# All half units of float64 weights loaded as 128 rows, through more staging slots

## The chip, the cores and the metric

The kernel runs on one core of one Trainium2 chip. The core has TensorE (matmuls), VectorE, ScalarE and GpSimd (elementwise work), SyncE (SP here, which issues most transfers) and 16 DMA engines. In the profile they are called PE (with PEld for the weight loads of TensorE), DVE, ACT, POOL and SP. Instructions of one engine run in the order in which they stand on it. The metric is the device time of one launch in microseconds, the median of several runs; lower is better.

## What is computed

Three layers in a row, in float32, for 8 batches of 576 tokens with 8 heads of 64:

```python
a = softmax over the sequence of phi            # 32 memory slots per head
k_m, v_m = a^T @ k, a^T @ v
x = softmax(q @ k_m^T / 8) @ v_m                # attention on the slots
h = x @ moe_w_in                                # 4608 x 512 times 512 x 2048
x = (h * sigmoid(1.702 * h)) @ moe_w_out        # 2048 x 512
# then, by token, the expert e of 8 with the highest logit of x @ w_gate:
y = gate * sigmoid(x @ w_output_gate)[e] * (relu(x @ w1[e]) @ w2[e])
```

`moe_w_in` and `moe_w_out` come as float64, which the inputs' making leaves them in; the kernel reads their bytes and makes float32 of them itself. All other inputs are float32.

## The kernel before

Tokens lie in 16 halves of 288 columns, two for each batch, written (b, hf). The first feed-forward layer is cut into 16 **units** (`u` or `f`, 128 of the 2048 hidden columns each). One **step** is one unit for one half: six matmuls into `h` (`ffn_h`), a tanh gate on ScalarE and VectorE with a split of the result `g` into a rounded part and a rest (lines 367 to 370), and twelve matmuls into four accumulators `acc` (`ffn_out`); every product is made of three matmuls with such split operands. `emit_h` runs two steps ahead of `emit_out` (`LOOK`). The output projection of attention is folded into the weights of each batch (`project`, lines 341 to 346).

The list `steps` begins with four early segments, in which halves (0,0), (0,1), (1,0) and (1,1) go through units 0 to 5 (`CUT`); each ends with `evac` (lines 387 and 389) and a store of the partial sums, `partd`. Then each of the four halves goes through units 6 to 15, then come the other batches with all 16 units, then the expert layer, whose weights `w2` (float32) are loaded two ahead by `load2` and split by `split2`.

The float64 weights come in 32 **half units** of 128 x 2048 16-bit words, 512 KB each, numbered in the order in which they are loaded. `conv_load(n)` issues the load of half unit n on SP. `conv_slot(n)` converts n and n + 1: ScalarE takes the top words (line 195, one instruction for each of the two), VectorE builds the exponent and the mantissa and adds them (lines 196 to 212); for n % 4 of 2 or more, which holds `moe_w_out`, the raw tile itself takes the result, ScalarE rounds it (214) and GpSimd makes the rest (215). So raw tiles of n % 4 below 2 come free with line 211 on VectorE, the others with line 215 on GpSimd. Of the slots from 24 on, the temporaries are three tiles named `phi0`, `phi1` and `c0` in turn. Slot n must be done before the step of its units; `conv` paces the slots at 0.8 half units a step.

The raw words are read from a byte offset of one word, so that the last row of the last half unit would end one word behind the array; half unit 31 is therefore loaded as 127 rows (line 181) and one row of 2047 words (line 183).

Where raw tiles lie: half units 0 to 11 in four places of the buffers that later hold the units of group 2 (`stage(2, 2 + n % 4)`, called `wb_123` in the rows below), 12 to 31 in a ring of three tiles `stg`. The ring also takes the keys and values of the batches from 2 on, and later `w2`. The keys and values of batch 1 lie in group 3 (`stage(3, c)`, `wb_119`), which is taken by units 12 to 15 only later; group 3 also holds temporaries of the slots below 24. `conv_slot` ends with the loads ahead:

```python
        while loaded[0] < min(NV, n + (6 if n + 5 < NR else 5)):
```

The order on each engine is not the order of the code: a list scheduler of the program's framework moves instructions forward or back on their engine. It also adds the waits for data and for free buffers.

Of the kernel before, what the change touches and what calls it, by code (L numbers as in the profile page):

```python
# [37 lines left out]
OUT_SHAPE = (N, DM)  # L38
CH = [(0, 128), (128, 128), (256, 128), (384, 128), (512, 64)]
LOOK = 2  # L40
LEAD = 8
FE = 60
CV0 = (0, 4, 8)
NR, NT = 12, 24
O1, R1, OQ, RQ, OR, RR = 0, 0.5, 6, 0.4, 9, 0.6
S1 = 32
ORDER = 'p k0 k1 c0 k2 k3 c1 k4 q0 c2 w q1'
# [5 lines left out]
def tile_kernel(ctx: ExitStack, tc: tile.TileContext, phiT, kv, qT, w1, w2, wg, out):  # L53
    nc = tc.nc
    PS = bass.MemoryType.PSUM
    w1 = w1.bitcast(U16).rearrange("u a p n -> (u a p n)")

    const = ctx.enter_context(tc.tile_pool(name="const", bufs=1))
    sb = ctx.enter_context(tc.tile_pool(name="sb", bufs=2))
# [88 lines left out]
    def load_kv(b, c):  # L148
        s0, n = CH[c]
        if b < 2:  # L150
            t = stage(2, 6) if (b, c) == (0, 4) else stage(3, c)
        else:
            t = sb.tile([128, 1024], F32, name="stg", bufs=3)
        nc.sync.dma_start(out=t[:n], in_=kv[b, s0:s0 + n])
        kv_t[b, c] = t

# [15 lines left out]
    def conv_load(n):  # L172


        if n < NR:
            raw_t[n] = stage(2, 2 + n % 4).bitcast(U16)
        else:
            raw_t[n] = sb.tile([128, 2048], U16, name="stg", bufs=3)
        o = (2 * (2 * (n // 4) + n % 2) + n % 4 // 2) * 128 * 2048 + 1
        rows = 128 if n < NV - 1 else 127  # L180
        nc.sync.dma_start(out=raw_t[n][:rows], in_=w1[o:o + rows * 2048].rearrange("(p n) -> p n", p=rows))
        if rows < 128:
            nc.sync.dma_start(out=raw_t[n][rows:, :2047], in_=w1[o + rows * 2048:o + 128 * 2048 - 1].rearrange("(p n) -> p n", p=1))

    def conv_slot(n):


        if n < NT:
            top, t = (stage(3, 5 + (n + i) % 6 / 2, 512).bitcast(U16) for i in range(2))
        else:  # L190
            top, t = (sb.tile([128, 1024], U16, name=("phi0", "phi1", "c0")[(n + i) % 3], bufs=1) for i in range(2))
        raw = [raw_t.pop(n + i) for i in range(2)]
        tops = [x.rearrange("p (n b) -> p n b", b=4)[:, :, 2] for x in raw]
        for i in range(2):
            nc.scalar.activation(out=t.bitcast(BF16)[:, 512 * i:512 * i + 512], in_=tops[i].bitcast(BF16), func=AF.Abs)
        nc.vector.tensor_scalar(out=t.bitcast(BF16), in0=t.bitcast(BF16), scalar1=WLO, scalar2=WHI,
                                op0=ALU.max, op1=ALU.min)
        nc.vector.tensor_scalar(out=t, in0=t, scalar1=3, scalar2=0x3FFF,
                                op0=ALU.logical_shift_left, op1=ALU.bitwise_and)
        for i in range(2):  # L200
            h = slice(512 * i, 512 * i + 512)
            nc.vector.scalar_tensor_tensor(out=top[:, h], in0=tops[i], scalar=0xC000, in1=t[:, h],
                                           op0=ALU.bitwise_and, op1=ALU.bitwise_or)
        nc.vector.tensor_scalar(out=t, in0=top, scalar1=0xFF80, scalar2=None, op0=ALU.bitwise_and)
        for i in range(2):
            h = slice(512 * i, 512 * i + 512)
            u = 2 * (n // 4) + i
            wa, wb = (x[:, u % 4] for x in group(u // 4, "A"))
            m = raw[i].bitcast(U32).rearrange("p (n b) -> p n b", b=2)[:, :, 0]
            w = wa if n % 4 < 2 else m.bitcast(F32)  # L210
            nc.vector.scalar_tensor_tensor(out=w, in0=m, scalar=2.0 ** -36, in1=t.bitcast(BF16)[:, h], op0=ALU.mult, op1=ALU.mult)
            nc.vector.tensor_add(out=w, in0=w, in1=top.bitcast(BF16)[:, h])  # L212
            if n % 4 >= 2:
                nc.scalar.copy(out=wb[:, 512:1024], in_=w)  # L214
                nc.gpsimd.tensor_sub(out=wb[:, 1024:1536], in0=w, in1=wb[:, 512:1024].bitcast(F32))
                u_t[u] = (wb[:, 0:256], wb[:, 256:512]), (wb[:, 512:1024], wb[:, 1024:1536])
        while loaded[0] < min(NV, n + (6 if n + 5 < NR else 5)):
            conv_load(loaded[0])
            loaded[0] += 1

# [1 line left out]
    stg_t = {}  # L222

    def load2(key, src):
        stg_t[key] = sb.tile([128, 1024], F32, name="stg", bufs=3)
        nc.sync.dma_start(out=stg_t[key], in_=src)

    def split2(key, slot):
# [354 lines left out]
    def slot_tasks():  # L583
# [39 lines left out]
        def g(i):  # L623
            p = misc([128, 4, SLOT], 1 - i)
            for j in range(4):
                nc.tensor.transpose(p[:, j], st["h"][:, i, j], ident)
            t = sb.tile([128, 2, 4, SLOT], F32R, name="stg", bufs=3)
            nc.scalar.copy(out=t[:, 0], in_=p)
            nc.vector.tensor_sub(out=t[:, 1], in0=p, in1=t[:, 0].bitcast(F32))
            st["g", i] = t  # L630
# [50 lines left out]
    def spread(step, thunks, every=1):  # L681
        for i, t in enumerate(thunks):
            put(int(step + i * every), t)
# [50 lines left out]
    def attn_tasks():  # L734
        for b in range(B):
# [8 lines left out]
            if b + 1 < B:  # L744
# [13 lines left out]
                else:  # L758
                    put(O1, lambda n=n: load_phi(n), lambda n=n: load_q(n, 0))
                    for c in range(5):  # L760
                        put(O1, lambda n=n, c=c: load_kv(n, c))
                    spread(O1, cm, R1)
                    spread(O1 + OQ, q0, RQ)

    def project_tasks():
# [111 lines left out]
def host(q, k, v, phi, moe_w_in, moe_w_out, moe2_w_gate, moe2_w_output_gate, moe2_w1, moe2_w2):  # L877
# [14 lines left out]
        a = wi.reshape(KD, 128, f, 128).transpose(2, 1, 0, 3).reshape(f, 128, 512)  # L892
        return np.concatenate([a, wo.reshape(f, 128, 512)], axis=2)

    w1 = c(units(moe_w_in, moe_w_out).reshape(NF1, 128, 2, 512).transpose(0, 2, 1, 3)).view(np.int64)
    w2 = c(np.stack([units(moe2_w1[e], moe2_w2[e]) for e in range(E)]))
    wg = c(np.concatenate([moe2_w_gate, moe2_w_output_gate], axis=1).reshape(KD, 128, 16).transpose(1, 0, 2))
    return dict(phiT=phiT, kv=kvp.reshape(B, S, H * 2 * D), qT=qTp, w1=w1, w2=w2, wg=wg)
# [21 lines left out]
```

## Time and profile before

| | |
|---|---|
| median of three runs | 1280.32 us (1278.87 to 1280.46) |
| profiled execution, its own time | 1287.78 us |
| its span, first to last instruction | 1286.1 us |
| mean granted clock of TensorE | 0.963 of full |

The rows that follow further below come from the profiled execution. A row of the timeline has start and duration in us, engine, line, operation, output <- input, and in brackets how long the engine sat idle before it and what ended that. "x12" means so many instructions in one merged row. L12 is line 12 of the kernel before; of the changed kernel, lines from 176 on are one to nine further down.

### The profile page before, as it was taken

What the parts mean: (1) busy time and instruction counts of PE and PEld (TensorE: products, weight loads), DVE (VectorE), ACT (ScalarE), POOL (GpSimd) and SP (SyncE); (2) the same over time, 40 slices, a digit from 0 to 9 for tenths busy, and PEclk for the clock granted to TensorE, in tenths of its full rate; (3) what the DMA queues carried; (4) which work ended last, traced back from release to release, by engine and by line L of the source; (5) the groups of instructions that cost most, each with busy time, mean ns of one, the idle gap of its engine ahead of it and who ended that gap; (6) DMA issues with size and microseconds to landing.
All of it is one profiled execution on the core that took longest, in us unless ns stands there. A gap on an engine that the chain in (4) does not pass through costs nothing. (4 is left out here: it accounts for less than half of the span.)

```text
span 1286.1 us, 24689 instructions
## 1 busy us (share of the span) xinstructions
PE 1196.4 (93%) x9628; PEld 1107.5 (86%) x9628; DVE 742.4 (58%) x2011; ACT 497.7 (39%) x1144; POOL 133.9 (10%) x137
## 2 busy tenths in 40 slices
PE   4689737999999999999999999999999999999996
PEld 2478626888988988999889889989999999999995
DVE  5898726576466467466556546676463553544521
ACT  3445414344444444443443444553242332332410
POOL 1221000020100100101101102001110001001100
PEclk8689967999999999999999999999999999999998
DMA  8534313433311311401311310475453443534300
GB/s 297 193 107 122 131 63 95 126 80 88 108 42 56 112 39 56 130 20 56 130 38 38 119 31 20 107 230 150 130 162 95 136 156 85 171 103 123 116 23 22
DMA packets 77017, 132.00 MB, mean 103 GB/s; under 512 B 12738, under 2 KB 49730, under 8 KB 76898
## 3 DMA queue, kind: packets, MB, share of 16 engines
q1 hardware_dynamic: 75170, 130.25, 33.2%
q8 instruction: 76, 1.25, 0.4%
q14 instruction: 43, 0.35, 0.1%
q0 software_dynamic: 1728, 0.15, 0.1%
HBM read 99.65 MB, written 31.12 MB: 102 GB/s over the span
## 5 line engine op out<-in xcount | busy, mean ns | idle before, releaser
L352 PE MATMUL acc<-g,wb 128*128 128x288 f32 x4608 | 690.1, 298 | 13.5 <-ACT wb L214 6.2
L352 PEld LDWEIGHTS acc<-g,wb 128*128 128x128 f32 x4608 | 642.6, 191 | 22.1 <-ACT g L369 6.8
L352 PE MATMUL h<-x,wb 128*128 128x288 f32 x2560 | 478.0, 305 | 36.6 <-DVE g L370 24.2
L352 PEld LDWEIGHTS h<-x,wb 128*128 128x128 f32 x2560 | 386.4, 191 | 86.1 <-issue 30.7
L367 ACT ACTIVATE th<-h 128x288 f32<-128x288 f32 x256 | 105.0, 411 | 122.0 <-PE h L352 121.4
L352 PE MATMUL h<-x,wa 128*128 128x288 f32 x512 | 151.5, 296 | 0.0
L369 ACT CAST g<-th 128x288 fp32r<-128x288 f32 x196 | 84.9, 433 | 171.2 <-PE acc L352 149.0
L370 DVE TENSOR_TENSOR g<-th,g 128x288 fp32r<-128x288 f32 x196 | 88.8, 453 | 100.2 <-ACT g L369 99.9
L368 DVE SCALAR_TENSOR_TENSOR th<-th,h 128x288 f32<-128x288 f32 x196 | 87.8, 448 | 75.5 <-ACT th L367 74.6
L373 DVE SCALAR_TENSOR_TENSOR g<-h,g 128x288 fp32r<-128x288 f32 x128 | 58.0, 453 | 117.3 <-ACT g L372 116.9
L231 ACT CAST wb<-stg 128x1024 fp32r<-128x1024 f32 x72 | 75.6, 1050 | 105.5 <-PE acc L352 90.4
L372 ACT ACTIVATE g<-h 128x288 fp32r<-128x288 f32 x128 | 52.2, 408 | 162.9 <-PE acc L352 162.0
L352 PEld LDWEIGHTS h<-x,wa 128*128 128x128 f32 x512 | 96.8, 189 | 0.0
L232 DVE TENSOR_TENSOR wa<-stg,wb 128x512 fp32r<-128x512 f32 x72 | 51.5, 715 | 77.4 <-ACT wb L231 76.9
L578 POOL TENSOR_TENSOR rt<-rt,scl 128x1152 f32<-128x1152 f32 x15 | 33.6, 2241 | 352.5 <-DVE rt L404 252.4
L330 POOL TENSOR_TENSOR x<-sf,x 128x288 fp32r<-128x288 f32 x32 | 25.9, 808 | 420.7 <-ACT x L329 394.4
L514 POOL DMA_INDIRECT listd<-ids,pos x48 | 45.5, 948 | 188.8 <-DVE ssm L321 67.4
L233 DVE TENSOR_TENSOR wb<-stg,wb 128x512 fp32r<-128x512 f32 x72 | 57.0, 792 | 0.0
L341 PE MATMUL m<-wa,kvc 64*32 64x512 f32 (+1 forms) x592 | 42.2, 576 | 10.7 <-DVE wa L212 9.3
L346 DVE TENSOR_TENSOR wb<-m,wb 128x512 fp32r<-128x512 f32 (+1 forms) x74 | 42.3, 608 | 15.7 <-ACT wb L345 15.7
L345 ACT CAST wb<-m 128x512 fp32r<-128x512 f32 (+1 forms) x74 | 35.6, 529 | 17.9 <-PE m L341 17.7
L369 ACT CAST g<-h 128x288 fp32r<-128x288 f32 x60 | 23.9, 398 | 46.6 <-PE acc L352 30.0
(200 smaller groups left out, 811.1 us busy)
## 6 DMA issues: line engine op xcount, KB each, us to landing
stg<-in_w_dram SPq DMA_DIRECT2D x91, 512.0 KB, 4.0
stg<-in_kv_dram SPq DMA_DIRECT2D x24, 512.0 KB, 4.0
x2d<-x SPq DMA_DIRECT2D x16, 576.0 KB, 5.9
x2tok<-rt SPq DMA_DIRECT2D x64, 144.0 KB, 2.9
x<-x2d SPq DMA_DIRECT2D x16, 576.0 KB, 4.0
out_dram<-rt SPq DMA_DIRECT2D x64, 144.0 KB, 2.8
q<-in_qT_dram SPq DMA_DIRECT2D x15, 576.0 KB, 3.9
wb<-in_w_dram SPq DMA_DIRECT2D x12, 512.0 KB, 4.8
```

What stands on the lines that cost most here:

```text
L231: nc.scalar.copy(out=wb[:, 0:1024], in_=stg)
L232: nc.vector.tensor_sub(out=wa, in0=stg[:, 0:512], in1=wb[:, 0:512].bitcast(F32))
L233: nc.vector.tensor_sub(out=wb[:, 1024:1536], in0=stg[:, 512:1024], in1=wb[:, 512:1024].bitcast(F32))
L346: nc.vector.tensor_sub(out=lo, in0=p[e], in1=hi.bitcast(F32))
L352: nc.tensor.matmul(p, lhsT=w[a][:, c0:c0 + 128], rhs=x[c], start=(first and i == 0), stop=(last and i == 2))
L367: nc.scalar.activation(out=t, in_=p, func=AF.Tanh, scale=0.851)
L368: nc.vector.scalar_tensor_tensor(out=o, in0=t, scalar=1.0, in1=p, op0=ALU.add, op1=ALU.mult)
L369: nc.scalar.copy(out=g[:, 0], in_=o)
L370: nc.vector.tensor_sub(out=g[:, 1], in0=o, in1=g[:, 0].bitcast(F32))
L372: nc.scalar.activation(out=g[:, 0], in_=p, func=AF.Relu)
L373: nc.vector.scalar_tensor_tensor(out=g[:, 1], in0=p, scalar=0.0, in1=g[:, 0].bitcast(F32), op0=ALU.max, op1=ALU.subtract)
L514: nc.gpsimd.indirect_dma_start(out=listd, out_offset=bass.IndirectOffsetOnAxis(ap=st["pos"][:, c:c + 1], axis=0), in_=ids[:, 2 * b * NJ + ...
```

## The change

All half units are loaded with 128 rows by one transfer. For that the host appends one word of float64 (a copy of the first) to the weights, so the last row can be read to its end; line 183 goes. The ring `stg` has four tiles instead of three (`NS`). Half units 0 to 15 now go through the places of group 2 (`NR` 16 instead of 12), 16 to 19 through the places of group 3 that held the keys and values of batch 1, and 20 to 31 through the ring. Loads from 16 on may be written out from step 5 on, when that batch's keys and values have been used (`free`); at that point all up to 23 are issued at once.

```diff
+NS = 4
-NR, NT = 12, 24
+NR, NT = 16, 24
...
-    w1 = w1.bitcast(U16).rearrange("u a p n -> (u a p n)")
+    w1 = w1.bitcast(U16)
...
         if n < NR:
             raw_t[n] = stage(2, 2 + n % 4).bitcast(U16)
+        elif n < NR + 4:
+            raw_t[n] = stage(3, n % 4).bitcast(U16)
         else:
-            raw_t[n] = sb.tile([128, 2048], U16, name="stg", bufs=3)
+            raw_t[n] = sb.tile([128, 2048], U16, name="stg", bufs=NS)
         o = (2 * (2 * (n // 4) + n % 2) + n % 4 // 2) * 128 * 2048 + 1
-        rows = 128 if n < NV - 1 else 127
-        nc.sync.dma_start(out=raw_t[n][:rows], in_=w1[o:o + rows * 2048].rearrange("(p n) -> p n", p=rows))
-        if rows < 128:
-            nc.sync.dma_start(out=raw_t[n][rows:, :2047], in_=w1[o + rows * 2048:o + 128 * 2048 - 1].rearrange("(p n) -> p n", p=1))
+        nc.sync.dma_start(out=raw_t[n], in_=w1[o:o + 128 * 2048].rearrange("(p n) -> p n", p=128))
...
-        while loaded[0] < min(NV, n + (6 if n + 5 < NR else 5)):
+        conv_loads(n + 6)
+
+    def conv_loads(n):
+
+        while loaded[0] < (min(NV, max(n, NR + 4 + NS)) if "free" in raw_t else min(n, NR)):
             conv_load(loaded[0])
             loaded[0] += 1
...
                     spread(O1, cm, R1)
+                    put(O1 + 5, lambda: raw_t.update(free=True), lambda: conv_loads(done[0] + 4))
...
-    w1 = c(units(moe_w_in, moe_w_out).reshape(NF1, 128, 2, 512).transpose(0, 2, 1, 3)).view(np.int64)
+    w1 = units(moe_w_in, moe_w_out).reshape(NF1, 128, 2, 512).transpose(0, 2, 1, 3).reshape(-1)
+    w1 = np.concatenate([w1, w1[:1]]).view(np.int64)
```

In the other places where the ring is named, `bufs=3` becomes `bufs=NS`.

The scheduler then orders the engines otherwise in the part where weights are converted. On SP, from the loads after batch 1's keys and values on, there stood before (`wb_123` are places of group 2, `stg` is the ring):

```order
L120 DMA listd<-x_525 128x288
L181 DMA stg<-in_w_dram 128x2048 x2
L181 DMA wb_123<-in_w_dram 128x2048 x2
L181 DMA stg<-in_w_dram 128x2048 x3
L704 DMA partd_0_102<-ev 128x1152
L162 DMA q<-in_qT_dram 128x1152
```

and in the changed kernel, with `wb_119` for group 3:

```order
L121 DMA listd<-x_525 128x288
L183 DMA stg<-in_w_dram 128x2048 x2
L183 DMA wb_123<-in_w_dram 128x2048 x2
L183 DMA stg<-in_w_dram 128x2048 x2
L183 DMA wb_123<-in_w_dram 128x2048 x4
L183 DMA wb_119<-in_w_dram 128x2048 x4
L708 DMA partd_0_102<-ev 128x1152
L163 DMA q<-in_qT_dram 128x1152
```

Before, the seven loads are half units 12 and 13, 10 and 11, 14 to 16. Now there are fourteen ahead of the first store of partial sums: 20 and 21, 10 and 11, 22 and 23, then 12 to 15 and 16 to 19, each behind the release of its place.

On ScalarE, around the steps of units 4 and 5 of the first early segment, there stood before (L367 and L369, the tanh and the cast of `g`; L258, copies for batch 1's attention):

```order
L367 ACTIVATE th<-h 128x288
L258 COPY et<-m_601 128x256
L367 ACTIVATE th<-h 128x288
L258 COPY et<-m_617 128x256
L369 CAST g<-h 128x288
L258 COPY et<-m_655 128x256
L369 CAST g<-h 128x288
L258 COPY et<-m_668 64x256
L367 ACTIVATE th<-h 128x288
L369 CAST g<-h 128x288
```

and now:

```order
L373 CAST g<-h 128x288
L262 COPY et<-m_615 128x256
L371 ACTIVATE th<-h 128x288
L262 COPY et<-m_653 128x256
L195 ACTIVATE wa_118<-wb_123 128x512
L373 CAST g<-h 128x288
L262 COPY et<-m_666 64x256
L195 ACTIVATE wa_118<-wb_123 128x512
L371 ACTIVATE th<-h 128x288
L195 ACTIVATE wa_118<-wb_119 128x512
L373 CAST g<-h 128x288
```

Three first operations on half units (14, 15 and 16, at L195) have moved in among the casts and activations of these steps.

On ScalarE around the last evacuation of the early segments (L389 before) there stood before:

```order
L195 ACTIVATE phi_1436<-stg 128x512
L367 ACTIVATE th<-h 128x288
L389 ACTIVATE ev<-acc_1284 128x288
L389 ACTIVATE ev<-acc_1286 128x288
L369 CAST g<-h 128x288
L367 ACTIVATE th<-h 128x288
L214 CAST wb_1097<-stg 128x512
L345 CAST wb_1097<-m_1574 128x2x128
L214 CAST wb_1097<-stg 128x512
```

and now (L393 is that evacuation):

```order
L195 ACTIVATE phi_1430<-stg 128x512
L373 CAST g<-h 128x288
L195 ACTIVATE phi_1430<-stg 128x512
L371 ACTIVATE th<-h 128x288 x2
L393 ACTIVATE ev<-acc_1278 128x288
L393 ACTIVATE ev<-acc_1280 128x288
L214 CAST wb_1099<-stg 128x512 x2
L373 CAST g<-h 128x288
L349 CAST wb_1099<-m_1479 128x2x128
L349 CAST wb_1099<-m_1480 128x2x128
L373 CAST g<-h 128x288
L195 ACTIVATE phi_1548<-stg 128x512 x2
```

Both first operations of slot 24 (half units 24 and 25) now stand ahead of the evacuation, where before the one of 25 stood twelve instructions behind it; those of slot 26 follow after four casts and the two of slot 22 (L214).

## Rows read from the trace of the kernel before

**Rows 1.** The page: the span, and TensorE's busy time with the other engines'.
```profile
span 1286.1 us, 24689 instructions
PE 1196.4 (93%) x9628; PEld 1107.5 (86%) x9628; DVE 742.4 (58%) x2011; ACT 497.7 (39%) x1144; POOL 133.9 (10%) x137
```
**Rows 2.** Windows: length, busy us of PE, PEld, DVE, ACT, POOL; clock, DMA share, GB/s.
```profile
80.00:140.00 60.00, 54.44 (x439) 48.29 (x439) 53.19 (x125) 30.80 (x77) 8.84 (x8) 0.97 0.40 132
140.00:210.00 70.00, 36.35 (x242) 31.26 (x241) 35.14 (x75) 19.05 (x43) 7.70 (x6) 0.73 0.29 92
...
400.00:600.00 200.00, 199.44 (x1732) 181.31 (x1732) 124.14 (x406) 88.25 (x223) 19.17 (x22) 1.00 0.24 72
```
**Rows 3.** TensorE's waits, 20 to 215 us, then 80 to 138: total, times, longest.
```profile
PE h L352 <- DVE g L370: 24.2, 5, 18.9
...
PE h L352 <- DVE g L370: 4.4, 3, 2.1
```
**Rows 4.** Timeline of the tail: ScalarE, then VectorE and SP.
```profile
137.88 0.41 ACT L389 ACTIVATE ev<-acc 128x288 f32<-128x288 f32 x1
...
155.11 0.74 ACT L195 ACTIVATE phi<-stg 128x512 bf16<-128x512 bf16 x1 [1.95 <-DVE wa L212]
...
164.07 0.65 ACT L195 ACTIVATE c<-stg 128x512 bf16<-128x512 bf16 x1
168.48 0.67 ACT L195 ACTIVATE c<-stg 128x512 bf16<-128x512 bf16 x1 [3.75 <-DMA stg<-in_w_dram]
174.43 0.67 ACT L195 ACTIVATE phi<-stg 128x512 bf16<-128x512 bf16 x1 [5.28 <-DVE wa L212]
...
195.76 0.65 ACT L195 ACTIVATE phi<-stg 128x512 bf16<-128x512 bf16 x1 [19.39 <-DMA stg<-in_w_dram]
...
201.09 1.29 DVE L212 TENSOR_TENSOR stg<-stg,phi 128x512 f32<-128x512 f32 x2
...
173.01 8.59 SPq L183 DMA_DIRECT2D stg<-in_w_dram  x1
```
**Rows 5.** Windows: the same columns, while half unit 31 is on its way.
```profile
185.00:190.00 5.00, 0.00 (x0) 0.00 (x0) 0.00 (x0) 0.00 (x0) 0.00 (x0) 0.50 0.06 26
```
**Rows 6.** Line 181, issue to landing: all; issued 150 to 168; half units 12, 13.
```profile
DMA to landing us min/median/max: 3.5/4.8/11.5
...
DMA to landing us min/median/max: 3.5/3.8/4.2
...
DMA to landing us min/median/max: 7.5/7.8/8.2
```
**Rows 7.** Timeline: slot 26 on VectorE (first and last), its casts, GpSimd for slot 22.
```profile
157.54 0.43 DVE L196 TENSOR_SCALAR phi<-phi 128x1024 bf16<-128x1024 bf16 x1 [0.41 <-ACT phi L195]
...
162.18 1.29 DVE L212 TENSOR_TENSOR stg<-stg,c 128x512 f32<-128x512 f32 x2
...
162.90 1.26 ACT L214 CAST wb<-stg 128x512 fp32r<-128x512 f32 x2 [1.32 <-DVE stg L212]
...
142.77 2.58 POOL L215 TENSOR_TENSOR wb<-stg,wb 128x512 fp32r<-128x512 f32 x2 [19.08 <-ACT wb L214]
```
**Rows 8.** Timeline: output matmuls of TensorE at the lower and at the full clock.
```profile
164.99 5.40 PE L352 MATMUL acc<-g,wb 128*128 128x288 f32 x22 [0.53 <-POOL wb L215]
...
209.88 1.76 PE L352 MATMUL acc<-g,wb 128*128 128x288 f32 x12
```
**Rows 9.** Timeline of the first early segment: VectorE, GpSimd, then ScalarE.
```profile
62.96 1.29 DVE L211 SCALAR_TENSOR_TENSOR wa<-wb,wa 128x512 f32<-128x512 uint32 x2
...
70.32 4.05 POOL L215 TENSOR_TENSOR wb<-wb,wb 128x512 fp32r<-128x512 f32 x2 [10.32 <-ACT wb L214]
...
73.87 0.41 ACT L369 CAST g<-h 128x288 fp32r<-128x288 f32 x1
...
77.63 0.40 ACT L369 CAST g<-h 128x288 fp32r<-128x288 f32 x1 [1.19 <-PE acc L352]
...
80.24 0.85 ACT L389 ACTIVATE ev<-acc 128x288 f32<-128x288 f32 x2
```

More of the change, by code (lines that the diff above doesn't have):

```diff
@@ L152, in load_kv @@
         else:
-            t = sb.tile([128, 1024], F32, name="stg", bufs=3)
+            t = sb.tile([128, 1024], F32, name="stg", bufs=NS)
         nc.sync.dma_start(out=t[:n], in_=kv[b, s0:s0 + n])
@@ L224, in load2 @@
     def load2(key, src):
-        stg_t[key] = sb.tile([128, 1024], F32, name="stg", bufs=3)
+        stg_t[key] = sb.tile([128, 1024], F32, name="stg", bufs=NS)
         nc.sync.dma_start(out=stg_t[key], in_=src)
@@ L626, in g @@
                 nc.tensor.transpose(p[:, j], st["h"][:, i, j], ident)
-            t = sb.tile([128, 2, 4, SLOT], F32R, name="stg", bufs=3)
+            t = sb.tile([128, 2, 4, SLOT], F32R, name="stg", bufs=NS)
             nc.scalar.copy(out=t[:, 0], in_=p)
```

## The prediction

> **What bounds the kernel now.** I read the page first for the shares [rows 1]: TensorE is busy 93% of the span, so it is the bound on the whole; what can be won is where it stands still. The windows by stage say where that is [rows 2]: from 400 to 600 us it is busy 199.4 of 200 us at the full granted clock (the stages after it look alike), but only 54.4 of 60 us from 80 to 140 and 36.4 of 70 us from 140 to 210, there at a mean clock of 0.73. So the loss lies ahead of 210 us, while weights are still being converted, and what is taken out there reaches the end undiminished. Next the waits of that stretch [rows 3]: the longest of TensorE is 18.9 us for `g` from VectorE. The timeline shows what it stands behind [rows 4]: ScalarE's row at L195 for half unit 31 (the last) starts at 195.76 after 19.39 us of waiting for a load of weights, and ScalarE's work behind it, the activations of two steps, starts only then. While it waits, the DMA engines show a busy share of 0.06, one of sixteen, at 26 GB/s [rows 5]; the other loads of the same line land in 3.5 to 11.5 us with a median of 4.8 [rows 6]. The one thing that sets the late load apart is its 127 rows, with a remainder of one row, whose issue alone holds SP 8.6 us.
>
> I write "slot n" for the conversion of half units n and n+1, and T0 for the first evacuation (L389) of the fourth early segment, at 137.88 [rows 4]. From T0 on ten steps of half 0 of batch 0 follow, with units 6 to 15, and their end waits for slot 30.
>
> **The tail, from T0 to the end of slot 30.** In before slot 30's last VectorE operation ends at 201.09 + 1.29 = 202.38, which is T0 + 64.5. In the changed program I work it out anew.
>
> The load of 31 now has 128 rows like the others, so its 19.39 us go. That alone would not be all: in before slot 28 also waited 3.75 us for half unit 29, since with three slots it can be issued only when slot 26 has been read by GpSimd; and slot 24 came late, its second L195 after T0. In the order of after, both L195 of slot 24 stand ahead of T0 on ScalarE, and after T0 VectorE has left of it one TENSOR_SCALAR and the two pairs of L211 and L212: about 0.4 + 1.3 + 1.3, with two evacuations between, T0 + 4.
>
> What is late next is the load of 26 and 27. They take the ring's slots of 22 and 23, whose last reader is GpSimd at L215. By the order that work starts behind T0: two evacuations of 0.4 us on ScalarE, half of a 1.26 us pair of casts, then 2.58 us for two subtractions [rows 7], so 27 can be issued at T0 + 0.8 + 0.7 + 2.6 = T0 + 4.1; with 0.3 for the issue and 3.8 for landing (the median of the four loads between 150 and 168 us [rows 6]) and 0.7 for its L195, VectorE can start slot 26 at T0 + 9. So this load is a new wait of some 4 to 5 us on ScalarE, and `g` for the next step is queued behind it; I count it in full.
>
> A slot's chain on VectorE takes from 157.54 to 162.18 + 1.29, 5.9 us with the steps' operations between [rows 7]. Slot 26 then ends at T0 + 14.9. From there the slots are a serial chain, because three temporaries (`phi0`, `phi1`, `c0`) go round and each slot's second is the one before's result: the period is 6.0 + 0.7 = 6.7 us where the load was there (from 168.48 to 174.43 with the first L195) and 9.0 us where casts lay between (155.11 to 164.07) [rows 4, 7]. I take 7.7, about midway, as both kinds follow each other. Slot 28 ends at T0 + 22.6, slot 30 at T0 + 30.3. Loads 28 and 29 wait for slot 24 alone, 30 and 31 for GpSimd after slot 26, at about T0 + 19; landed by T0 + 23.4, they come just when ScalarE wants them. Against T0 + 64.5 the tail is **34.2 us shorter**; with the period at its ends (2.0 less or 2.6 more for two of them) and a landing of 3.5 to 4.8 us [rows 6], 30.6 to 36.5. TensorE itself permits it: twelve output matmuls take 1.76 us at full clock [rows 8], 0.147 each, so ten steps of 18 are 26 us, and some 30 with the projections that the order puts between them. The clock can add to the gain, up to 2 us, as the last two steps in before ran at half level.
>
> **The first stretch, up to T0.** Here the change costs. In before, half units 12 and 13 were fetched at 42.7 us into a free ring slot; now 12 to 15 go to group 2 again and wait for the slots of 8 to 11. Load 12 waits for slot 8's L211, at 62.96 + 0.7; it lands at about 68, and ScalarE stands at its L195. Loads 14 and 15 wait for GpSimd's pair from 70.32 to 74.37 [rows 9], a little later as 12 delays the pair (1 us): released at 73 and 75, landed at 77 and 79.5. By the order the L195 of 14 now stands ahead of a cast of `g` that in before ran at 73.87, that of 16 ahead of one that ran at 77.63. So the cast at 73.87 moves to about 78, and the one at 77.63 to 80.7 (16 landing soon behind 15) or to 84.5 (if four loads in a row take 7.5 to 8.2 us, as two loads behind others did [rows 6]). On SP, the transfers queued behind these waiting loads are 17 to 19, the `partd` store and the next `q`; none is wanted before the evacuation at 80.24. I take that evacuation 5 us later (4 to 7).
>
> From there to T0 nothing waits for a load: 16 to 23 are all in. In before TensorE lost 5.6 of 60 us between 80 and 140 [rows 2]. But VectorE is busy 53.2 of these 60, and by the order it has slot 24, 5.9 us, to do in part there besides. I give back 2 of the 5, so T0 is **3 us later** (from 2 earlier, 4 less all of the 5.6, to 9 later, 7 and a third of slot 24).
>
> By the Trainium skill it would be a little less: its page "DMA: Bandwidth & Descriptors", section "Anatomy of one DMA", puts a transfer at 2.0 us plus its bytes at 436 GB/s, an estimate of 3.2 us for 512 KB, though for transfers issued from GpSimd. The row of this case has 3.8 for the tail and the sum goes by that; by the page the wait for 27 and that for 15 would be 0.6 us shorter each.
>
> **The rest.** Two w2 loads ahead stay two loads ahead, so the fourth ring slot is worth nothing in the expert half by the order of issue; TensorE is full there [rows 2]. The appended word costs no instruction. Loads are as many as before, less the one-row remainder.
>
> **Sum.** -34.2 + 3 = -31 us. The profiled execution took 1287.78 us around a span of 1286.1; it would take 1256.6. The median of the three runs, 1280.32, is 7.5 us below that execution; shifted alike, 1249.
>
> **Rivals.**
> - *Only the 128 rows pay.* Load 31, issued just ahead of the row at 173.01 [rows 4], would land 3.8 us later instead of 23: -19. The ring's share of 15 is eaten if the period is 9.0, load 27 takes 7.8 us to land as 12 and 13 did [rows 6] and T0 comes 9 us late: -34.2 + 2.6 + 4 + 9 = -19, so 1261, from 1258 to 1264. For it speaks that VectorE has little room from 80 to 140; against it that the load waits of that stretch do go.
> - *The clock falls in the tail.* From 80 to 140 us the granted clock was 0.97 on the mean [rows 2] with no wait of TensorE above 2.1 us [rows 3]; in the tail with its long waits it was 0.73, and there, at the lower level of 1.2 GHz, 22 output matmuls took 5.40 us, 0.245 each, against 0.147 [rows 8]. Were all ten steps at the lower level, their 30 us would be about 50 and bind, where the forecast ends them some 5 us behind slot 30, at T0 + 35: 15 us of the gain go, 1264; with half of them at it, 40 us, 1254. The page "TensorE: Matmul & The Clock Gate" of the Trainium skill, section "Part 1: The HAM clock gate", says the slow level is the default and only activity lifts it; by that rule bursts parted by load waits stay slow. Against it: the one wait that I find is of 4 to 5 us, and TensorE is two steps behind ScalarE there.
> - *Slower: each load of the first stretch is waited for alone.* Loads 12 to 19 are eight; if ScalarE stood before each for a whole landing, 8 x 4.8 = 38 us [rows 6], it would give back more than 34.2 and end at about 1284. It decides from 4.3 us a load on. Against it: 16 to 19 are released by TensorE nearly together.
> - *The change doesn't do what it says:* the late landing is not from the 127 rows. Then only the ring's 15 less 3 to 9 are left, 1268 to 1274. The share of one engine in sixteen [rows 5] speaks against it.
> - *More:* no new wait at 26 and 27 and T0 not late, -39 to -43: 1237 to 1241.
>
> **How the numbers follow.** Chances: forecast (1242 to 1258) 0.63; only the 128 rows 0.16; clock 0.08; more 0.06; no 128-row effect 0.04; slower 0.03. Predicted 1249. The range for 8 in 10 takes the forecast, most of the first rival and part of the second: 1240 to 1264. About 0.2% (2.6 us) is what a measurement of this kernel can tell from no change; within it lies no case but what falls between the fourth rival and the third, 0.02; slower 0.03; faster 0.95.
>
> **What the profile after would show.** No wait of ScalarE at L195 above 6 us; no window with a DMA share of 0.06; the issue line of one row gone. The first evacuation of the first segment at 84 to 87 instead of 80.24, T0 at 137 to 147, slot 30's last L212 some 30 us behind T0, and a wait of 4 to 5 us for half unit 26 or 27. It is wrong if T0 is beyond 147, if the span from T0 to slot 30 is above 36, or if the stages behind 210 us no longer have TensorE 99% busy.

## The result

The changed kernel takes **1247.26 us** in the median (1244.70 to 1248.71, 4 runs), the kernel before, on the same chip, 1279.86 us (1278.87 to 1280.46, 4 runs). The ratio is 0.9744, with a 95% interval from 0.9726 to 0.9762: 32.6 us, or 2.6%, faster. The prediction said 1249, with 1240 to 1264 as its range.

The profiled execution of the changed kernel took 1248.71 us around a span of 1247.0. Against the profiled execution of before (span 1286.1 [rows 1]) that is 39.1 us less, more than the medians differ by. Some of it is that one execution of before: a kernel with nothing but a wider last row (the third experiment) is as fast as before in the median, and its span was 1281.1. I read places in the traces to about 3 us, and totals from the medians: in before and in kernels 1, 3 and 4 below, whose engines do the same work in the same order up to T0, T0 lies between 134.5 and 137.9.

### Profile after

First the page of the changed kernel, its span and its engines, to be held against [rows 1]:

```profile
span 1247.0 us, 24667 instructions
PE 1186.2 (95%) x9628; PEld 1099.6 (88%) x9628; DVE 742.0 (59%) x2011; ACT 497.5 (40%) x1144; POOL 134.0 (11%) x137
```

The matmuls, and VectorE's and ScalarE's instructions, are as many as before; TensorE's share of the span went from 93 to 95%. Where that came from is in the windows by stage (columns as in [rows 2]):

```profile
80.00:140.00 60.00, 54.91 (x461) 49.62 (x460) 58.05 (x134) 32.51 (x79) 11.65 (x10) 1.00 0.27 95
140.00:210.00 70.00, 63.86 (x548) 56.56 (x547) 49.54 (x126) 30.87 (x78) 5.16 (x4) 0.98 0.38 121
400.00:600.00 200.00, 200.00 (x1762) 181.01 (x1762) 119.65 (x374) 89.39 (x227) 17.61 (x20) 1.00 0.27 83
```

From 140 to 210 us TensorE is busy 63.9 us instead of 36.4, at a mean granted clock of 0.98 instead of 0.73. From 400 to 600 nothing is left to win, as in before. New is VectorE's share: 58 of 60 us in the first window, where it was 53.2.

Then what ScalarE waits for at line 195 from 60 to 180 us (total, times, longest), all groups there are:

```profile
ACT phi L195 <- DVE wa L212: 7.8, 2, 5.8
ACT wb L195 <- DMA wb<-in_w_dram: 5.2, 1, 5.2
ACT wa L195 <- DMA wb<-in_w_dram: 1.5, 1, 1.5
ACT phi L195 <- DMA stg<-in_w_dram: 1.1, 1, 1.1
ACT wa L195 <- DVE wa L211: 1.1, 1, 1.1
ACT wa L195 <- DVE wb L211: 1.1, 2, 0.7
```

The 19.39 us for half unit 31 and the 3.75 us for 29 [rows 4] are gone, with no load wait in the tail at all. The largest load wait left is 5.2 us, for half unit 12. The longest wait of the tail is now for VectorE's L212, the end of the slot before.

Last the timeline: T0 (lines have shifted, 389 is 393 and 369 is 373), the tail's L195 on ScalarE, and the last L212 of slots 22 to 30 on VectorE:

```profile
132.91 0.42 ACT L393 ACTIVATE ev<-acc 128x288 f32<-128x288 f32 x1
...
142.09 1.22 ACT L195 ACTIVATE phi<-stg 128x512 bf16<-128x512 bf16 x2 [5.81 <-DVE wa L212]
...
151.19 0.69 ACT L195 ACTIVATE c<-stg 128x512 bf16<-128x512 bf16 x1
152.04 0.70 ACT L195 ACTIVATE c<-stg 128x512 bf16<-128x512 bf16 x1
...
159.11 1.29 ACT L195 ACTIVATE phi<-stg 128x512 bf16<-128x512 bf16 x2 [1.95 <-DVE wa L212]
...
132.73 1.29 DVE L212 TENSOR_TENSOR stg<-stg,wa 128x512 f32<-128x512 f32 x2
140.77 1.28 DVE L212 TENSOR_TENSOR wa<-wa,phi 128x512 f32<-128x512 f32 x2
148.98 1.29 DVE L212 TENSOR_TENSOR stg<-stg,c 128x512 f32<-128x512 f32 x2
157.79 1.28 DVE L212 TENSOR_TENSOR wa<-wa,phi 128x512 f32<-128x512 f32 x2
166.51 1.29 DVE L212 TENSOR_TENSOR stg<-stg,phi 128x512 f32<-128x512 f32 x2
```

T0 is at 132.91 instead of 137.88, and slot 30 ends at 166.51 + 1.29 = 167.80 instead of 202.38 [rows 4]: 34.6 us earlier, 5.0 of them ahead of T0 and 29.6 behind it.

### The profile page after: what moved, and what is told of

It reads as the page before. It is cut to its first block, busy times and chain, and to the rows that moved or that the text cites. A ratio compares the mean times of both kernels' runs of the same rounds, so it can differ in the third digit from the quotient of the medians.

```text
span 1247.0 us, 24667 instructions
## 1 busy us (share of the span) xinstructions
PE 1186.2 (95%) x9628; PEld 1099.6 (88%) x9628; DVE 742.0 (59%) x2011; ACT 497.5 (40%) x1144; POOL 134.0 (11%) x137
## 5 line engine op out<-in xcount | busy, mean ns | idle before, releaser
L373 ACT CAST g<-th 128x288 fp32r<-128x288 f32 x196 | 84.7, 432 | 171.2 <-PE acc L356 150.0
L374 DVE TENSOR_TENSOR g<-th,g 128x288 fp32r<-128x288 f32 x196 | 88.6, 452 | 99.2 <-ACT g L373 98.6
L372 DVE SCALAR_TENSOR_TENSOR th<-th,h 128x288 f32<-128x288 f32 x196 | 87.8, 448 | 76.1 <-ACT th L371 75.2
```

Source lines behind the costliest of these rows:

```text
L372: nc.vector.scalar_tensor_tensor(out=o, in0=t, scalar=1.0, in1=p, op0=ALU.add, op1=ALU.mult)
L373: nc.scalar.copy(out=g[:, 0], in_=o)
L374: nc.vector.tensor_sub(out=g[:, 1], in0=o, in1=g[:, 0].bitcast(F32))
```

## The experiments

Ratios are to the kernel before, measured beside each kernel; a difference from the changed kernel is the ratio less 0.9744, times 1280 us. The intervals are 0.3 to 0.6% wide, so differences from the changed kernel of under 3 us are not resolved. "Slot 30" is the end of its last L212 in the profiled execution.

| kernel | median us | ratio (95%) | T0 | slot 30 |
|---|---|---|---|---|
| before | 1279.86 | 1 | 137.88 | 202.38 |
| changed | 1247.26 | 0.9744 (0.9726 to 0.9762) | 132.91 | 167.80 |
| 1: 128 rows alone | 1262.66 | 0.9864 (0.9832 to 0.9896) | 134.47 | 178.25 |
| 2: ring and groups alone | 1264.78 | 0.9874 (0.9849 to 0.9899) | 132.66 | 185.39 |
| 3: 127 rows and one full row | 1280.55 | 0.9991 (0.9972 to 1.0009) | 137.17 | 201.10 |
| 4: 112, 15 and 1 rows | 1265.74 | 0.9875 (0.9847 to 0.9902) | 136.89 | 185.61 |
| 5: ring of three | 1256.84 | 0.9812 (0.9799 to 0.9825) | 131.33 | 173.42 |
| 6: group 2 not used again | 1254.48 | 0.9788 (0.9775 to 0.9802) | 143.41 | 175.35 |
| 7: addition on GpSimd | 1248.61 | 0.9746 (0.9733 to 0.9760) | 136.84 | 171.04 |
| 8: pace 0.9 | 1250.10 | 0.9758 (0.9739 to 0.9777) | 138.47 | 166.48 |
| 9: less on VectorE | 1275.00 | 0.9948 (0.9932 to 0.9963) | 130.59 | 156.54 |
| 10: evacuations on ScalarE | 1246.88 | 0.9731 (0.9708 to 0.9755) | 137.05 | 166.34 |
| 11: subtraction on VectorE | 1246.58 | 0.9733 (0.9710 to 0.9756) | 135.29 | 170.96 |
| 12: 10 and 11 together | 1244.39 | 0.9719 (0.9705 to 0.9732) | 130.48 | 167.00 |

My theory was the prediction's: the late load of half unit 31, late because of its 127 rows, and the ring's wait for the next loads are two separate costs. The rivals were that one part carries all, and that the load is late for another reason. The first four kernels decide this.

### 1 and 2. Each half of the change alone

Kernel 1 is before with the appended word and the single load:

```diff
-        rows = 128 if n < NV - 1 else 127
-        nc.sync.dma_start(out=raw_t[n][:rows], in_=w1[o:o + rows * 2048]...)
-        if rows < 128:
-            nc.sync.dma_start(out=raw_t[n][rows:, :2047], ...)
+        nc.sync.dma_start(out=raw_t[n], in_=w1[o:o + 128 * 2048].rearrange("(p n) -> p n", p=128))
```

> The kernel before with the appended word alone: the load of half unit 31 has 128 rows; ring of three, no group reused beyond what was. Theory (the late load and the ring are two separate costs): ScalarE's 19.39 us at L195 go, nothing else of the tail moves, the kernel is 19 us faster than before, about 1261, and half unit 31 lands in about 4 us instead of 23. The wait of 3.75 us for half unit 29 stays. Rival (the ring carries most of the gain): load 31 is replaced as the late one by the next, and less than 10 us are gained, 1270 or more. Second rival (the 128 rows alone carry nearly all): over 28 us faster, 1252 or less.

Kernel 2 is the changed kernel with the load in two pieces again, and without the appended word:

```diff
-        nc.sync.dma_start(out=raw_t[n], in_=w1[o:o + 128 * 2048].rearrange("(p n) -> p n", p=128))
+        rows = 128 if n < NV - 1 else 127
+        nc.sync.dma_start(out=raw_t[n][:rows], in_=w1[o:o + rows * 2048]...)
+        if rows < 128:
+            nc.sync.dma_start(out=raw_t[n][rows:, :2047], ...)
```

> The changed kernel with the last load in 127 rows and a remainder of one row again (no appended word): the ring of four and groups 2 and 3 alone. In the changed kernel load 31 is issued at 153.2 us and its L195 runs at about 160. Theory (two separate costs): with the old form it lands 23 us after its issue, at about 176, so ScalarE waits some 16 us there and the kernel takes 16 us more than the changed one, about 1263; the one-row issue holds SP about 8.6 us again. Rival (the late landing came from something else in that place, such as the other loads in flight): no wait above 6 us, the same time as the changed kernel, 1247.

Measured: 18.2 us less than before with the 128 rows alone (1262.66 against 1280.83 beside it), 16.1 us less with the ring and groups alone. Both of the theory's numbers stand, and 18 + 16 = 34 is close to the 32.6 of both together: each of the three differences is known to 2 to 4 us, and within that nothing is shared. The tail of kernel 1, ScalarE's L195 of half units 29 and 31:

```profile
164.09 0.67 ACT L192 ACTIVATE c<-stg 128x512 bf16<-128x512 bf16 x1 [3.87 <-DMA stg<-in_w_dram]
...
171.87 0.65 ACT L192 ACTIVATE phi<-stg 128x512 bf16<-128x512 bf16 x1 [1.17 <-DMA stg<-in_w_dram]
```

The wait for 31 is 1.17 us, that for 29 is still 3.87. In kernel 2, SP's issues of half unit 31 and ScalarE's L195 of it, then the window ahead of that:

```profile
152.89 0.30 SPq L184 DMA_DIRECT2D stg<-in_w_dram  x1
153.25 8.66 SPq L186 DMA_DIRECT2D stg<-in_w_dram  x1
...
176.82 0.65 ACT L198 ACTIVATE phi<-stg 128x512 bf16<-128x512 bf16 x1 [17.29 <-DMA stg<-in_w_dram]
```

```profile
170.00:176.00 6.00, 0.00 (x0) 0.00 (x0) 0.00 (x0) 0.00 (x0) 0.00 (x0) 0.50 0.06 26
```

The load is issued 20 us earlier than in before (172.65) and takes 24 us (23 in before), at the same 26 GB/s and the same share of 0.06: the lateness goes with the load, not with the place in the program.

### 3 and 4. What of this load is late

Kernel 3 is before with the appended word and a full row in place of the short one:

```diff
-            nc.sync.dma_start(out=raw_t[n][rows:, :2047], in_=w1[... - 1]...)
+            nc.sync.dma_start(out=raw_t[n][rows:], in_=w1[...]...)
```

> The kernel before with its last load still in two pieces, 127 rows and one row, but the one row full: 2048 words instead of 2047. Theory (the 127 rows make the load late, since they move at the rate of one DMA engine in sixteen): nothing changes, ScalarE still waits about 19 us, a DMA share of 0.06 stands in the same place, 1280 as before. Rival (the short row of 2047 words, whose issue holds SP 8.6 us, makes it late): the wait goes, 1261. The issue of the full row may still get cheaper without a change of the time.

Kernel 4 is before with the 127 rows cut in two:

```diff
-        rows = 128 if n < NV - 1 else 127
+        parts = ((0, 128),) if n < NV - 1 else ((0, 112), (112, 127))
+        for r0, r1 in parts:
+            nc.sync.dma_start(out=raw_t[n][r0:r1], ...)
...
```

> The kernel before with its last load in three pieces: 112 rows, 15 rows and the short row of 2047 words. Theory (127 rows go to one DMA engine in sixteen because of their number): the 112 rows land in about 4 us; the 15 rows, if all on one engine, need about 15/127 of 19 us plus the fixed part, some 4 to 6 us; the wait of ScalarE falls from 19.4 to 1 to 5 us and the kernel is 14 to 19 us faster, 1261 to 1266. Rival (the short row makes it late): the wait stays at 19 us, 1280.

Measured: 1280.55 and 1265.74, as the theory of the 127 rows had it. SP and ScalarE in kernel 3, then in kernel 4:

```profile
171.52 8.71 SPq L183 DMA_DIRECT2D stg<-in_w_dram  x1
...
194.50 0.65 ACT L195 ACTIVATE phi<-stg 128x512 bf16<-128x512 bf16 x1 [19.62 <-DMA stg<-in_w_dram]
```

```profile
170.26 0.87 SPq L182 DMA_DIRECT2D stg<-in_w_dram  x2
171.18 0.22 SPq L184 DMA_DIRECT2D stg<-in_w_dram  x1
...
177.41 0.66 ACT L196 ACTIVATE phi<-stg 128x512 bf16<-128x512 bf16 x1
```

With 112 and 15 rows, ScalarE does not stand at the load of half unit 31, though the short row is still there. So the 127 rows alone were the cause, and the same gain as by padding is to be had, to about 3 us, by cutting the load at a multiple of 16. The two rows on SP say one thing more: the one-row transfer holds SP 8.7 us even when the row is full, and 0.22 us when it is short but stands behind other pieces. The hold belongs to the 127-row transfer ahead of it, and not to the row, to which I had put it down.

The Trainium skill has the rule, in "DMA: Bandwidth & Descriptors", section "Why a DMA increments its semaphore by 16 and not by 1": the number of engines is the largest up to 16 that divides the slowest dimension of both access patterns, so that 127 rows go to one. The share of one in sixteen, in the traces of before and of kernels 2 and 3, agrees, and so does kernel 4.

### 5 and 6. How many buffers the tail and the first stretch need

Both start from the changed kernel. Kernel 5:

```diff
-NS = 4
+NS = 3
```

> The changed kernel with a ring of three slots instead of four; groups 2 and 3 and the 128 rows stay. Theory (the fourth slot is needed in the tail): half units 29 and 31 wait for a load again, 3.9 and 1.2 us in the kernel that has the 128 rows alone, so this one is 3 to 8 us slower than the changed kernel, 1250 to 1255. Rival (VectorE, busy 31.4 of 35 us from 133 to 168 us, sets the tail and hides the load waits): within 2 us of the changed kernel. Second rival (the reuse of groups 2 and 3 is worth nothing, the fourth slot all): as slow as the 128 rows alone, 1262.

Kernel 6:

```diff
-NR, NT = 16, 24
+NR, NT = 12, 24
```

> The changed kernel with half units 12 to 15 in group 3 and those from 16 on in the ring of four, so that none of them waits for the slots of 8 to 11. Theory (the wait of 5.21 us for half unit 12 and of 1.7 us for two others costs the first stretch what I put in the prediction): the first evacuation of the first segment comes 2 to 4 us earlier than 81.1, and the kernel is 1 to 4 us faster than the changed one, 1243 to 1246. Rival (VectorE, busy 58 of 60 us from 80 to 140 us, absorbs it): the first evacuation moves, T0 stays within 1 us and the time is the same. Slower if the eight loads, issued together at 41 us, delay the transfers that the first stretch wants.

Kernel 5 is 0.0068 x 1280 = 8.7 us slower than the changed kernel, just above the theory's range. ScalarE's L195 of half unit 29 waits as in kernel 1:

```profile
159.28 0.68 ACT L195 ACTIVATE c<-stg 128x512 bf16<-128x512 bf16 x1 [3.81 <-DMA stg<-in_w_dram]
```

Its slot 30 ends 5.6 us later than the changed kernel's, with T0 1.6 us earlier, so the fourth slot of the ring pays for itself in the tail, by load waits, in spite of VectorE's high share there. That is nearly all by which the two profiled executions differ (spans of 1252.9 and 1247.0); what the medians show beyond it is not in these traces.

Kernel 6 missed on both sides: neither faster nor the same, but 5.6 us slower. My reading of its code was wrong first of all: half units 12 to 15 could not be issued at 41 us, since group 3 holds keys and values until later; they went out together from 72 us. The first evacuation came at 80.72, 0.4 us earlier than the 81.12 of the changed kernel. Counted from the tanh near 50 us it is 2.0 us earlier (29.3 us against 31.3), but in kernels 2 and 5, which do the same as the changed kernel up to there, it is 30.1 and 29.4. So what the wait of 5.2 us for half unit 12 costs the first segment is not resolved, and is 2 us at most. What the kernel lost is behind that: 16 to 19 now come through the ring, and ScalarE waits for loads again between 80 us and T0, which came 10.5 us later. The waits at L195 for loads to the ring in kernel 6 (total, times, longest), and the window:

```profile
ACT wa L195 <- DMA stg<-in_w_dram: 4.0, 2, 2.3
ACT phi L195 <- DMA stg<-in_w_dram: 2.7, 2, 2.4
```

```profile
80.00:143.00 63.00, 55.97 (x436) 48.27 (x436) 54.52 (x126) 30.39 (x76) 9.89 (x10) 0.95 0.30 109
```

VectorE is idle 63.00 - 54.52 = 8.5 us there, 7.0 more than in the changed kernel up to its T0 (below); another 3.0 us are five operations that it does more. This showed me what to look for in the two kernels of the case, up to T0 in each. The kernel before, its waits at L195 for loads and the window:

```profile
ACT wa L195 <- DMA stg<-in_w_dram: 4.6, 3, 3.0
ACT wb L195 <- DMA stg<-in_w_dram: 1.9, 1, 1.9
```

```profile
80.00:138.00 58.00, 52.44 (x424) 46.29 (x424) 51.19 (x121) 29.68 (x74) 8.84 (x8) 0.97 0.42 137
```

The changed kernel, in which one load wait of 1.1 us is left there, and its tail:

```profile
80.00:133.00 53.00, 49.73 (x417) 45.52 (x416) 51.48 (x121) 29.48 (x72) 8.86 (x8) 1.00 0.26 93
133.00:168.00 35.00, 27.04 (x233) 22.56 (x231) 31.39 (x67) 16.25 (x41) 5.37 (x5) 0.95 0.43 140
```

Up to T0, VectorE has 121 operations and 51 us of work in both, and needs 58 us for it in before and 53 in after. The 5.3 us of its idle time that are gone answer to 6.5 us of load waits on ScalarE that are now 1.1. It is no matter of one execution: from the first evacuation to T0 it is 57.6 us in before and 55.9 to 57.0 in kernels 1, 3 and 4, but 51.8 in the changed kernel and in kernel 2 and 51.9 in kernel 5. TensorE's clock is 1.00 there in after and 0.97 in before; the runs don't separate that from the waits.

### 7 to 12. What binds the stretch now

VectorE, busy 51.5 of 53 us and then 31.4 of 35, was the new suspect; the rival was the chain of the three temporaries, on which each slot waits for the one before it. Kernel 7 moves half of the additions to GpSimd:

```diff
-            nc.vector.tensor_add(out=w, in0=w, in1=top.bitcast(BF16)[:, h])
+            (nc.gpsimd if n % 4 < 2 else nc.vector).tensor_add(out=w, in0=w, in1=top.bitcast(BF16)[:, h])
```

> The changed kernel with the addition of L212 on GpSimd instead of VectorE for the first slot of each pair (n modulo 4 below 2). Theory (VectorE's busy time sets the stretch from 80 to 168 us): about 1.29 us less work on VectorE for four or five slots, up to 5 us faster than the changed kernel, 1242 to 1246. Rival (the serial chain of the temporaries sets it, not the busy time): GpSimd takes about 1.3 us for one such operation against 0.65 on VectorE, so each of these slots, 24 and 28 in the tail among them, has a chain 1.3 us longer: 2 to 5 us slower.

Neither: 1248.61, no difference from the changed kernel. The page says why it could not gain; VectorE's busy time did not fall, though 16 operations left it (2011 to 1995):

```profile
PE 1188.9 (95%) x9628; PEld 1101.3 (88%) x9628; DVE 741.9 (59%) x1995; ACT 497.4 (40%) x1144; POOL 155.0 (12%) x153
```

And the timeline of kernel 7, GpSimd first, then VectorE:

```profile
134.78 2.76 POOL L215 TENSOR_TENSOR wb<-stg,wb 128x512 fp32r<-128x512 f32 x2 [5.40 <-ACT wb L214]
...
134.87 0.46 DVE L372 SCALAR_TENSOR_TENSOR h<-th,h 128x288 f32<-128x288 f32 x1
135.23 1.13 DVE L196 TENSOR_SCALAR phi<-phi 128x1024 bf16<-128x1024 bf16 x1
136.40 1.42 DVE L198 TENSOR_SCALAR phi<-phi 128x1024 uint16<-128x1024 uint16 x1
```

L196 and L198 take 0.42 us each elsewhere (the median of L198 is 0.42, of L196 too). Here they end 0.3 us behind GpSimd's first and second operation. So these operations are held where they meet one of GpSimd, and what is moved to GpSimd comes back as longer operations. Not all are held: the row of L372, one of whose inputs is `h` in PSUM, lies within GpSimd's first operation and takes its usual 0.46 us. Up to 210 us, 9 of the 10 operations of L196 and L198 that start beside one of GpSimd take 0.65 to 1.42 us; of the 25 of L372 and L374, the steps' own, none takes over 0.47. Kernel 11 is the reverse, GpSimd's work moved to VectorE:

```diff
-                nc.gpsimd.tensor_sub(out=wb[:, 1024:1536], in0=w, ...)
+                nc.vector.tensor_sub(out=wb[:, 1024:1536], in0=w, ...)
```

> The changed kernel with GpSimd's subtraction (L215, 16 pairs of operations of 1.3 us) on VectorE. With the addition on GpSimd instead, VectorE's busy time over the run had stayed at 741.9 us though 16 operations of 0.66 us had left it: its other operations got longer while GpSimd worked. Theory (an operation of VectorE that meets one of GpSimd is held until that ends, so GpSimd's work costs VectorE about its own price): VectorE's busy time rises by much less than the 21 us that 32 operations of 0.66 us make, 5 us or so, its operations of L196 and L198 are never above 0.7 us, and the time is within 3 us of the changed kernel. Rival (GpSimd's operations cost VectorE nothing): VectorE's busy time rises by 21 us and the kernel is 8 to 14 us slower.

It has 16 operations more on VectorE, not 32 as I wrote, 0.68 us each and so 10.9 us in all, and VectorE's busy time rose from 742.0 to 744.9 only:

```profile
PE 1188.6 (95%) x9628; PEld 1100.3 (88%) x9628; DVE 744.9 (60%) x2027; ACT 496.5 (40%) x1144; POOL 112.4 (9%) x121
```

So some 8 us of the 10.9 had been paid already. That is to be read to about 3 us, since kernels with the 2011 operations of the changed one have 741.2 (kernel 2) to 744.9 (kernel 8). All forms of L198 now have their longest within 0.01 us of 0.42 (min/median/max in ns; the changed kernel has one of 1390 and one of 1404 among its first two forms):

```profile
L198 DVE TENSOR_SCALAR wa<-wa x8: 414/417/422, 27.0 to 130.7; 128x1024 uint16<-128x1024 uint16 x8
L198 DVE TENSOR_SCALAR wb<-wb x4: 415/424/428, 17.6 to 114.7; 128x1024 uint16<-128x1024 uint16 x4
```

The time, 1246.58, is that of the changed kernel, as the theory had it.

Kernel 9 takes work off VectorE without giving it to another engine: the clamp and the mask.

```diff
-        nc.vector.tensor_scalar(out=t.bitcast(BF16), in0=t.bitcast(BF16), scalar1=WLO, scalar2=WHI,
-                                op0=ALU.max, op1=ALU.min)
...
-        nc.vector.tensor_scalar(out=t, in0=top, scalar1=0xFF80, scalar2=None, op0=ALU.bitwise_and)
```

> The changed kernel without two of VectorE's operations in every slot, the clamp of L196 and the mask of L204 (0.42 us each, so the converted weights are other numbers; everything else is as it was). Theory (VectorE's work, busy 51.5 of 53 us from 80 to 133 us and 31.4 of 35 us from there to 168, sets the end of the conversion): some ten slots fall in that stretch, 8 us less work, TensorE idles 11 us there at present, so 5 to 9 us faster than the changed kernel, 1240 to 1244. Rival (loads, or TensorE itself, set the end): within 2 us of the changed kernel, with new waits at L195 for loads.

Its total can't be used: with other weights the gate sends tokens elsewhere, and the kernel has 9688 matmuls instead of 9628. Ahead of the gate the work is the same but for the two operations, 13.4 us in 16 slots, though the scheduler orders it otherwise on every engine. Slot 30 ends at 156.54, 11.3 us earlier than in the changed kernel; the first evacuation, at 76.44, is already 4.7 us earlier. ScalarE's 24 evacuations of the later halves, in the changed kernel and in kernel 9 (first and last start):

```profile
L393 ACT ACTIVATE x<-acc x24: 411/412/413, 308.6 to 812.6; 128x288 f32<-128x288 f32 x24
```

```profile
L390 ACT ACTIVATE x<-acc x24: 405/412/416, 300.7 to 801.7; 128x288 f32<-128x288 f32 x24
```

The first is 7.9 us earlier and the last 10.9. This speaks for VectorE's work setting the end of the conversion, and not the loads: ScalarE waits for one load at L195 behind 80 us, 2.1 us where it was 1.1. What is taken out reaches the stages behind. What the new order does to it isn't separated, and the kernel doesn't tell busy time from the chain, since the two operations lie on both. Kernel 10 was to do that: it takes L391 off VectorE, which isn't in the chain.

```diff
-            if d % 2:
+            if d % 2 and not act:
...
-                evac(t, 0.5)
+                evac(t, 0.5, act=True)
```

> The changed kernel with all four evacuations of each early segment on ScalarE, instead of two of the four on VectorE (L391, 8 operations of 0.45 us, 3.6 us in all, between 81 and 140 us). It takes work from VectorE and leaves the serial chain of the temporaries as it is. Theory (busy time on VectorE binds): T0 or slot 30 up to 3 us earlier, 1244 to 1247. Rival (the chain binds, or the longer evacuation on ScalarE holds up the next segment's first output matmuls by 0.8 us each time): the same or up to 3 us slower.

Slot 30 ends 1.5 us earlier and T0 4.1 us later; the time, 1246.88, differs by less than can be resolved. That is inconclusive: I can't say which of the two binds, busy time or chain. Kernel 8 shifts the slots against the steps, by their pace:

```diff
-PB, PR = 6, 0.8
+PB, PR = 6, 0.9
```

> The changed kernel with the conversion paced at 0.9 slots for a step instead of 0.8 (PR): the same work, slots earlier against the steps. Theory (VectorE's work, busy 89.5 of 95 us from 80 to 168 us and over, sets the end of the conversion whatever the order): T0 later, the tail shorter by the same, the time within 3 us of the changed kernel. Rival (the place of the slots in the order matters, the tail's waits are what is left): 3 to 8 us faster, as slot 30 would end with the last step.

T0 comes 5.6 us later and slot 30 ends 1.3 us earlier; the time, 1250.10, is within 3 us, as the theory of a fixed amount of VectorE's work has it. Kernel 12 has the edits of 10 and 11 together, as their diffs above:

> The changed kernel with both edits that each ran within 1 us of it: all early evacuations on ScalarE and L215 on VectorE. Theory (VectorE binds the stretch up to slot 30, and the subtraction moved back costs it 3 us net where it had been held 7.6): the two do not add up to more than 3 us, 1244 to 1248. Rival (each has its own gain): 1243 or less, ratio to the kernel before at or below 0.970.

At 1244.39, within the theory's 1244 to 1248, it has the lowest median of all. Its interval, 0.9705 to 0.9732, just meets that of the changed kernel (0.9726 to 0.9762), so a gain of some 3 us is likely and not shown.

## Why the prediction came out, step by step

The sum, -31 us, was measured as -32.6, and its two parts, the late load and the ring with the groups, are shown by kernels 1 to 4. In the two profiled executions, from which the terms are read, the spans differ by 39.1: 34.6 up to slot 30 and 4.5 behind it, and kernel 3, as fast as before in the median, has a span 5.0 shorter than before's. Two of the terms were off, in opposite directions: the prediction had T0 at 140.9 and slot 30's end 30.3 behind it, at 171.2; they were at 132.9 (outside of the 137 to 147 that I had named) and 34.9 behind it, at 167.8.

- *The late load and its 127 rows:* right, by kernels 1 to 4. The rival that only this part pays put it at -19 and the ring at -15; the parts measured -18 and -16, and the ring's share was not eaten.
- *The first evacuation, 5 us later (4 to 7):* it came at 81.12, not at 84 to 87, and 0.9 us later than in before. At 50 us, where the program is the same, this execution was already 2.0 us ahead (a tanh at 49.82 that is at 51.83 in before), so the change cost about 2.9 in these two. Over the kernels that do the same up to there, it is 28.3 to 30.1 us from that tanh to the evacuation in before and kernels 1, 3 and 4, and 29.4 to 31.3 in the changed one and kernels 2 and 5: some 1 us later on the mean, and less than forecast in any case. The wait for 12 came, 5.2 us; those for 14 and 15 didn't, as GpSimd's pair came at 68.37 and took 2.74 us instead of 70.32 and 4.05 [rows 9].
- *2 us given back up to T0:* this is the step that failed. From the first evacuation to T0 it was 57.6 us in before and 51.8 in after: 5.8 given back. I had looked at TensorE's idle time and VectorE's high share, and not at what VectorE's idle 6.8 us of those 58 stood behind: four load waits of ScalarE, 6.5 us in all, that the earlier loads take away. Kernel 6 brings such waits back, and T0 is late again. With nearly all of them taken out, the first stretch gains and does not cost: T0 came 5.0 us earlier, 2.0 of them this execution's own, and not 3 later.
- *Slot 24 ends at T0 + 4:* it was T0 + 9.1. At 142.05 it ended 2.9 us earlier than I had forecast it on the clock. T0 was the wrong anchor: the slots go on at VectorE's pace, and where the evacuation falls between them matters little, as kernels 8 and 10 show.
- *A wait of 4 to 5 us for the load of 26 or 27:* not seen. Half unit 27 was issued at T0 + 4.6 (forecast T0 + 4.1) and landed 4.8 us later, at about the time that slot 24 ended; ScalarE's 5.81 us are put down to L212. The load was where I put it, but it was no longer alone.
- *A period of 7.7 us, 6.7 to 9.0:* 8.2, 8.8 and 8.7, near the upper end; VectorE is 90% busy there (31.39 of 35 us), so besides the chain its work may bind; the runs leave open which.
- *The clock:* the granted clock was 0.95 from 133 to 168 and 0.98 from 140 to 210, so this rival didn't come in. Where load waits stay in the tail, as in kernels 1 and 5, it was 0.85 from 140 to 210.
- *The rest:* the window from 400 to 600 is full in both, as said.

The errors, 8 us too late at T0 and 4.6 us too short behind it, cancel in part: that the forecast is nearer than its terms is luck. Had I taken all load waits out, which the range allowed for (T0 2 us earlier than in before), with a period of 9, the sum would have been -33.6.

## What to carry to other kernels

Look for a transfer like the 127 rows here: its signature is a window with a DMA share of 0.06, one engine in sixteen. Padding the array by a word, for 128 rows, gave 18 us, and cutting the load into 112 and 15 rows 15 us. When a load wait is taken out of a serial pipeline, add up all waits of that kind ahead of the place, not only the longest, and anchor the forecast on the engine that will be the bound afterwards (here, by kernel 9, more likely VectorE than the loads), not on an event that happens to lie near. Before work is moved from VectorE to GpSimd, look whether VectorE's short operations get longer where GpSimd runs, and which of them.

## What the runs showed of the hardware that I had not expected

- GpSimd's operations hold some of VectorE's. With 16 additions moved to GpSimd, VectorE's busy time stayed at 741.9 us; with 16 subtractions of 0.68 us moved to VectorE it rose by 2.9 us only. Operations of 0.42 us took up to 1.4. The Trainium skill tells of it in "SBUF — State Buffer", section "SBUF: two separate sides": the two engines share a port pair, and an operation of GpSimd, or one of VectorE in a 2-port mode or with two SBUF inputs (these only against one of GpSimd that reads SBUF), has it for the whole instruction, whichever starts first. The traces agree in that L372 and L374, with one input in PSUM, were not held in kernel 7; they don't show the port itself.
- The 127 rows also held the queue that issued the next transfer: SP stood 8.6 to 8.7 us at the one row behind them (2047 words in before and kernel 2, 2048 in kernel 3), and 0.22 us at the same row behind pieces of 112 and 15.
